# Attention and MLP with a gate on one core: statistics copied right behind their reciprocals, the fourth input tile loaded later, the gate finished a block sooner, the input transposes of two blocks moved to their ends

## The chip, the core and the metric

The kernel runs on one core of one Trainium2 chip. A core has five instruction queues: TensorE (PE: matmuls, with weight loads beside them), VectorE (DVE), ScalarE (ACT), GpSimd (POOL) and SyncE (SP, which here issues nearly all DMAs). Each queue works in the order in which its instructions stand; what one engine needs of another it waits for by a semaphore. The metric is the device time of one execution in microseconds (us), lower is better. Before the change three executions took 2256.01, 2258.34 and 2260.13 us, a median of 2258.34.

## What is computed

The reference takes x of 2048 tokens by 576 values, float32. A gate mixes two branches of the same x:

```python
g = sigmoid((x * gate_w).sum(-1, keepdims=True))
# A: softmax attention, 32 heads of 18 values
qkv = (x @ wqkv).reshape(B, S, 3, H, Dh)          # wqkv 576 x 1728
p = softmax(q @ k^T * Dh ** -0.5)
a = (p @ v) @ wo
# B: layer norm, then an MLP of 4608 hidden values
y = (x - mean(x)) / sqrt(var(x) + 1e-5)
b = gelu(y @ w1 + b1) @ w2 + b2
return g * a + (1 - g) * b
```

The kernel keeps float32 accuracy with matmuls on rounded operands: a tensor is split into a rounded high part (named hh, or the first of a pair) and the rest (hl), and each product is made of three matmuls.

## The kernel before

**Stages.** The program has three. The first, some 239 us, is the input stage, and most of the change lies in it: four blocks of 512 tokens (tb = 0 to 3), each with 17 steps (g = 0 to 16) on PE. Steps 0 to 8 are QK groups (qk_group: 14 matmuls of 128x512 into one PSUM tile, then ACT makes hh of it, L886, DVE makes hl, L887, and SP stores both in DRAM, L889 and L890). Steps 9 to 16 are V groups (v_group: 14 matmuls of 128x288; an even one's PSUM is evicted by ACT, an odd one's by DVE, L912, after which SP stores V, L915). The second stage is a loop of 512 steps over heads and key tiles, in which attention and MLP are interleaved on PE by a list of due times. The third, some 49 us, is the output projection (L1203), in four blocks.

**What each block prepares for the next.** While block tb runs, the tile of block tb+1 is loaded (load_x, L733 and L736, two buffers) and goes through these, each called behind the matmuls of one step:

- norm(tb+1, 0) and norm(tb+1, 1): means and variances on DVE (L846, L847), then at the end of the second a square root on ACT (L853) and two reciprocals on DVE (the last is L859), which gives the deviations, 128x4;
- stat_rows: the means and deviations are copied by DVE into one tile, stp (L825, L826), PE transposes it (L828), ACT copies the rows (L829) and SP writes them to DRAM (L830);
- load_wide: SP reads these rows back, spread over all partitions (L834), into a tile that the code calls wide and that the trace names qa;
- norm(tb+1, 2) and norm(tb+1, 3): DVE multiplies the tile by the gate's weights and sums (L866), for the gate;
- x_chunk 0 to 4: PE transposes 128 columns of the tile (L757); DVE subtracts the means (L772, which needs wide), ACT rounds the transposed part (L774), DVE makes the rest (L775); of the last chunk ACT makes two pieces (L778, L779) and DVE half a piece (L780); POOL multiplies by the deviations (L782). The next block's groups multiply with what L774 to L780 write (the tile big);
- y_parts: some steps after its chunk ("lag"), ACT and POOL split the normalized y (L797, L798), and SP stores it (L789, L791) for the MLP.

Block 0 does its own tile besides: norm(0, 0) and norm(0, 1) at g=3 and 4, the gate and the normalization in place at g=7 and 8, and its transposes y_chunk (L805, L806) at g=12 to 16. The weights of Q, K and V come in seven slices, loaded by SP (L743 to L745) and split by ACT and DVE or POOL (L751, L752) ahead of the groups that need them.

**The table of steps.** BLOCK (L59) gives for each of the first three blocks the step of each of these: stats, rows, wide, x (the first chunk), gate, load (of the tile after next) and the lag. PE's PSUM pool of this stage (ps_a) has four tiles, which turn in order. Between the steps stand rounds of attention scores for the loop's first unit (ROUNDS, L54): four matmuls (L227), each with a maximum on DVE (L229). In block 3 the gate is finished: ACT's exponential at g=9 (L988), three small operations of DVE at g=14 (L990 to L992).

**The output stage.** Each of its blocks of 512 tokens has eight half tiles. PLAN (L49) says behind which of them DVE and ACT do the seven pieces (normed 0 to 6) that prepare the block after it.

Of the kernel before, what the change touches and what calls it, by code (L numbers as in the profile page):

```python
# [11 lines left out]
ALU = mybir.AluOpType  # L12
# [35 lines left out]
TOTAL = NB * NG * (G // 2 * 27 * 231 + 8 * 3 * G * 131)  # L48
PLAN = [[(), (0,), (1,), (2,), (3,), (4,), (5, 6), ()], [(), (), (0,), (1,), (2,), (3,), (4,), (5, 6)],  # L49
        [(), (), (0,), (1,), (2,), (3,), (4,), (5, 6)]]  # L50
LAST = 28
# [6 lines left out]
N_AT = {3: 0, 4: 1, 7: 2, 8: 3}  # L58
BLOCK = [dict(stats=0, rows=4, wide=5, x=9, lag=3, gate=15, load=16),  # L59
         dict(stats=2, rows=5, wide=6, x=7, lag=2, gate=13, load=1),  # L60
         dict(stats=0, rows=3, wide=4, x=6, lag=2, gate=12)]
W_AT = {0: 1, 1: 2, 2: 3, 4: 4, 6: 5, 7: 6}
# [6 lines left out]
def gated_mix_kernel(ctx: ExitStack, tc: tile.TileContext, x, wqkv, wo, w1, b1, w2, b2, gate_w, out):  # L69
# [635 lines left out]
    with ExitStack() as a:  # L705
# [117 lines left out]
        def stat_rows(tb):  # L823

            nc.vector.tensor_copy(stp[:, 0:4], stats[:, 4 * tb:4 * tb + 4, 0])  # L825
            nc.vector.tensor_copy(stp[:, 4:8], rstds[tb])  # L826
            ps = psum(ps_a)
            nc.tensor.transpose(ps[:, :P], stp, ident)  # L828
            nc.scalar.activation(strow, ps[:8, :P], AF.Copy)  # L829
            nc.sync.dma_start(st_scr[tb], strow)  # L830
# [7 lines left out]
        def norm(tb, stage):  # L838
# [9 lines left out]
            if stage == 1:  # L848
# [9 lines left out]
                nc.vector.tensor_scalar(sd, sd, 0.5, None, op0=ALU.mult)  # L858
                nc.vector.reciprocal(rstd, sd)  # L859
            if stage >= 2:  # L860
                if stage == 2:
# [75 lines left out]
        for tb in range(NB):  # L937
            work = [(qk_group, (tb, mt)) for mt in (range(9) if tb < 2 else (4, 0, 1, 2, 3, 5, 6, 7, 8))] + [(v_group, (tb, t, n)) for t in range(4) for n in range(2)]
            for g, (fn, args) in enumerate(work):
# [34 lines left out]
                if tb == NB - 1:  # L974
# [7 lines left out]
                    if g == 9:  # L982
# [3 lines left out]
                        next(stream[0])  # L986

                        nc.scalar.activation(gate, glog, AF.Exp, scale=-1.0)  # L988
                    if g == 14:
                        nc.vector.tensor_scalar(gate, gate, 1.0, None, op0=ALU.add)  # L990
                        nc.vector.reciprocal(gate, gate)
                        nc.vector.tensor_scalar(gate1, gate, -1.0, 1.0, op0=ALU.mult, op1=ALU.add)  # L992
                    if g == 7:
# [8 lines left out]
                if tb == 2 and g == 10:  # L1002
                    for c0, c1 in ((0, 3), (3, 5)):
                        dma_r(nc.sync, low[0:64, c0:c1], y_scr[0, 1, c0:c1].rearrange("c p n -> p c n"))
                        defer(6, lambda c0=c0, c1=c1: nc.scalar.activation(low[64:128, c0:c1], low[0:64, c0:c1], AF.Copy))
                if tb == 2 and g == 4:
                    load_k(0, 2 * TB, 3 * TB)
# [310 lines left out]
```

## Time and profile before

The profiled execution took 2257.29 us, its span on the core 2255.4 us. Stretches of it, cut where PE's first matmul of a block stands; busy time is the sum of instructions, the clock is the mean that was granted to PE:

| stretch (us) | length | PE | DVE | ACT | POOL | PE clock | DMA share |
|---|---|---|---|---|---|---|---|
| start, 0 to 9.27 | 9.27 | 4.29 | 2.12 | 3.85 | 8.35 | 1.00 | 0.85 |
| block 0, to 68.08 | 58.81 | 51.80 | 38.08 | 25.78 | 22.56 | 0.94 | 0.75 |
| block 1, to 130.47 | 62.39 | 54.65 | 34.84 | 14.20 | 14.77 | 0.92 | 0.76 |
| block 2, to 188.12 | 57.65 | 55.73 | 42.62 | 15.57 | 12.72 | 1.00 | 0.54 |
| block 3, to 239.42 | 51.30 | 51.30 | 29.89 | 18.59 | 10.95 | 1.00 | 0.69 |
| loop, to 2206.60 | 1967.18 | 1958.28 | 1475.12 | 1343.23 | 934.25 | 1.00 | 0.42 |
| output, to 2255.40 | 48.80 | 44.10 | 25.46 | 7.37 | 0.00 | 1.00 | 0.54 |

A stretch in which PE is busy for its whole length is set by PE. In block 0 it is idle for 7.0 us, in block 1 for 7.7, in block 2 for 1.9. The quoted rows below come from three views. In the timeline a row has start, duration, engine, line, operation, out<-in, shapes and a count; in brackets the idle time of the engine before it and what ended it. In the list of waits a row has the total, the number and the longest. In the windows a row has the stretch, its length, busy time (with the number of instructions) of PE, its weight loads, DVE, ACT and POOL, then PE's clock, DMA's share and GB/s.

### The profile page before, as it was taken

How to read it: one execution, taken by the hardware profiler on the slowest of the kernel's cores; microseconds unless marked ns; L12 is line 12 of the kernel's file. 1: busy time of each engine (PE TensorE's matmuls, PEld its weight loads, DVE VectorE, ACT ScalarE, POOL GpSimd, SP SyncE). 2: the span in 40 equal slices, each digit the busy share in tenths (PEclk: the TensorE clock that was granted, in tenths of full speed). 3: DMA queues.
4: the chain of work that ended last, by engine and by line, in shares of the span. 5: the costliest groups of instructions: out<-in, count | busy, mean ns of one | idle time of the engine just before them, and what ended most of it. 6: DMA issues, size and time to landing. Idle time of an engine off the chain costs nothing.

```text
span 2255.4 us, 51587 instructions
## 1 busy us (share of the span) xinstructions
PE 2220.2 (98%) x20528; PEld 1582.7 (70%) x20528; DVE 1648.1 (73%) x2886; ACT 1428.6 (63%) x2653; POOL 1003.6 (44%) x1001
## 2 busy tenths in 40 slices
PE   8899999999999999999999999999999999999999
PEld 6777766767666767676667666676766767667668
DVE  5476677777777777777777777777776777777734
ACT  3322776777776666666666666666665666666772
POOL 3221756666665444444463444444444444444710
PEclk9999999999999999999999999999999999999999
DMA  8847654444456533333254423243364323342264
GB/s 236 261 165 242 213 175 154 149 143 153 139 193 174 160 103 117 115 128 122 99 154 138 167 99 120 100 139 103 116 172 149 106 99 113 109 131 94 100 220 166
DMA packets 164104, 329.23 MB, mean 146 GB/s; under 512 B 56814, under 2 KB 84074, under 8 KB 153134
## 3 DMA queue, kind: packets, MB, share of 16 engines
q1 hardware_dynamic: 161766, 322.19, 44.3%
q8 instruction: 162, 2.65, 0.5%
q10 hardware_dynamic: 1968, 3.70, 0.4%
q14 instruction: 80, 0.66, 0.1%
q0 software_dynamic: 128, 0.03, 0.0%
HBM read 233.47 MB, written 96.17 MB: 146 GB/s over the span
## 4 chain that ended last, share of the span: by engine, by line
PE 91%; DVE 4%; DMA 2%; ACT 1%; issue 1%; POOL 1%; SPq 0%; ACTq 0%; POOLq 0%; DVEq 0%
PE ps L285 20%; PE ps L484 19%; PE ps L572 19%; PE ps L267 13%; PE ps L227 10%; PE ps L880 3%; PE ps L1203 3%; DVE m L229 1%; PE ps L901 1%; DMA x<-in_B_w_dram 1%; ACT zz L537 0%; POOL w L180 0%; PE ps L757 0%; DMA qk_scr<-hh 0%; ACT p L270 0%
## 5 line engine op out<-in xcount | busy, mean ns | idle before, releaser
L229 DVE TENSOR_REDUCE m<-ps 128x1 f32<-128x512 f32 x2048 | 1312.4, 685 | 407.1 <-PE ps L227 383.2
L270 ACT ACTIVATE p<-ps 128x512 f32<-128x512 f32 x1368 | 741.8, 596 | 381.3 <-PE ps L267 376.8
L484 PE MATMUL ps<-big,w 64*128 64x512 f32 x3708 | 567.9, 393 | 1.9 <-ACT p L270 1.1
L180 POOL TENSOR_SCALAR zz<-zz 128x512 f32<-128x512 f32 x288 | 178.4, 620 | 748.9 <-ACT zz L537 734.0
L270 ACT ACTIVATE ring<-ps 128x512 f32<-128x512 f32 x680 | 369.1, 596 | 188.9 <-PE ps L267 186.3
L572 PE MATMUL ps<-w,hh 64*128 64x288 f32 x4352 | 483.3, 294 | 1.9 <-DVE x L589 0.9
L267 PE MATMUL ps<-qa,ka 56*128 56x512 f32 x2048 | 459.3, 421 | 3.5 <-ACT p L270 1.8
L572 PEld LDWEIGHTS ps<-w,hh 64*128 64x128 f32 x4352 | 424.0, 186 | 29.4 <-DVE x L589 3.0
L227 PE MATMUL ps<-ka,qa 54*128 54x512 f32 x2048 | 436.1, 398 | 0.9
L484 PEld LDWEIGHTS ps<-big,w 64*128 64x128 f32 x3708 | 368.2, 186 | 68.5 <-ACT p L270 1.4
L180 POOL TENSOR_TENSOR zz<-zz,z 128x512 f32<-128x512 f32 x288 | 371.8, 1291 | 24.0
L267 PEld LDWEIGHTS ps<-qa,ka 56*128 56x128 f32 x2048 | 213.0, 184 | 221.7 <-DVE m L229 181.8
L572 PE MATMUL ps<-w,hl 64*128 64x288 f32 x2176 | 347.6, 292 | 0.8 <-POOL hl L180 0.8
L285 PE MATMUL ps<-p,vt 128*32 128x512 f32 x2560 | 322.8, 598 | 0.0
L227 PEld LDWEIGHTS ps<-ka,qa 54*128 54x128 f32 x2048 | 218.8, 185 | 27.3 <-DVE m L229 7.3
L572 PEld LDWEIGHTS ps<-w,hl 64*128 64x128 f32 x2176 | 230.7, 184 | 1.2 <-POOL hl L180 1.1
L180 POOL TENSOR_TENSOR hl<-zz,hh 128x512 fp32r<-128x512 f32 x136 | 176.6, 1299 | 11.3
L180 POOL TENSOR_TENSOR w<-x,w 128x576 fp32r<-128x576 f32 (+1 forms) x54 | 98.8, 1844 | 171.5 <-ACT w L392 144.3
L285 PE MATMUL ps<-ring,vt 128*32 128x512 f32 x1280 | 168.7, 598 | 0.0
L285 PEld LDWEIGHTS ps<-p,vt 128*32 128x32 f32 x2560 | 67.0, 109 | 142.9 <-issue 136.6
L880 PE MATMUL ps<-big,wqk 128*128 128x512 f32 x432 | 110.4, 403 | 0.4 <-DVE wqk L752 0.4
L589 DVE SCALAR_TENSOR_TENSOR x<-ps,x 128x288 f32<-128x288 f32 x256 | 104.1, 449 | 8.6 <-PE ps L572 8.4
(124 smaller groups left out, 1497.8 us busy)
## 6 DMA issues: line engine op xcount, KB each, us to landing
w<-w_scr SPq DMA_DIRECT2D x54, 1152.0 KB
w<-w_scr SPq DMA_DIRECT2D x108, 576.0 KB
x<-in_B_w_dram SPq DMA_DIRECT2D x72, 288.0 KB
w_scr<-w SPq DMA_DIRECT2D x18, 1152.0 KB
w_scr<-w SPq DMA_DIRECT2D x36, 576.0 KB
qa<-qk_scr SPq DMA_DIRECT2D x192, 72.0 KB
ka<-qk_scr SPq DMA_DIRECT2D x84, 144.0 KB
qk_scr<-hh SPq DMA_DIRECT2D x36, 256.0 KB
```

Of the source, the lines that this page charges most:

```text
L180: fn(*args, **kw)
L227: nc.tensor.matmul(ps, qa[r0:r0 + 54, t * P:(t + 1) * P], ka[r0:r0 + 54, kb * TB:(kb + 1) * TB], start=True, stop=True)
L229: nc.vector.tensor_reduce(M4[u][:, h, t, kb:kb + 1], ps, axis=AX.X, op=ALU.max)
L267: nc.tensor.matmul(ps[h], ka[r0:r0 + 56, kc * P:(kc + 1) * P], qa[r0:r0 + 56, qb * TB:(qb + 1) * TB], start=True, stop=True)
L270: nc.scalar.activation(RING[n % 3][:, qb, h], ps[h], AF.Exp, scale=SCALE)
L285: nc.tensor.matmul(OB[u][r:r + 32, :], v[:, k, 19 * h:19 * h + 32], RING[c % 3][:, qb, h, :], start=(k == 0), stop=(k == NT - 1))
L484: nc.tensor.matmul(ps[h], wt[w_][r, c, :], y[r, c, :], start=(k == 0), stop=(k == 26))
L572: mm = nc.tensor.matmul(ps[nn][:, :ND], h_[r, tok], w_[p_][r, cs[nn]], start=(k == 0), stop=(k == 6 * G - 1))
L589: nc.vector.scalar_tensor_tensor(dst, ps[nn][:, :ND], 0.5, b2b[:, cs[nn]] if g == 0 else dst, op0=ALU.mult, op1=ALU.add)
L880: nc.tensor.matmul(ps, w_[:, c, ms], big[:, s_, :], start=(k == 0), stop=False)
L901: nc.tensor.matmul(ps[:, :ND], big[:, s_, tok], w_[:, c, cs], start=(k == 0), stop=False)
L1203: nc.tensor.matmul(ps[:, :ND], OT[b][2][:, s_, tok], w_part(w_, c)[:, cs], start=(k == 0), stop=(k == 13))
```

## The change

```diff
--- before.py
+++ after.py
@@ -46,8 +46,8 @@
 TAIL = (6, 12, 16, 20)
 BUSY = 20
 TOTAL = NB * NG * (G // 2 * 27 * 231 + 8 * 3 * G * 131)
-PLAN = [[(), (0,), (1,), (2,), (3,), (4,), (5, 6), ()], [(), (), (0,), (1,), (2,), (3,), (4,), (5, 6)],
-        [(), (), (0,), (1,), (2,), (3,), (4,), (5, 6)]]
+PLAN = [[(), (0,), (1,), (2,), (3,), (4,), (5, 6), ()], [(), (0,), (1,), (2,), (3,), (4,), (5, 6), ()],
+        [(), (), (0,), (1,), (2,), (3, 4), (5,), (6,)]]
 LAST = 28
 PSTEP = (489, 492, 495, 497)
 ORDER = (0, 1, 3, 2)
@@ -56,9 +56,9 @@
 SLOTS = [lambda g: 0, lambda g: 0, lambda g: int(g >= 4), lambda g: 1 if g < 9 else 2]
 SKIP = 0
 N_AT = {3: 0, 4: 1, 7: 2, 8: 3}
-BLOCK = [dict(stats=0, rows=4, wide=5, x=9, lag=3, gate=15, load=16),
-         dict(stats=2, rows=5, wide=6, x=7, lag=2, gate=13, load=1),
-         dict(stats=0, rows=3, wide=4, x=6, lag=2, gate=12)]
+BLOCK = [dict(stats=0, rows=3, wide=4, x=10, lag=4, gate=15, load=16),
+         dict(stats=6, rows=9, wide=10, x=12, lag=3, gate=8, load=10),
+         dict(stats=0, rows=3, wide=4, x=6, lag=3, gate=4)]
 W_AT = {0: 1, 1: 2, 2: 3, 4: 4, 6: 5, 7: 6}
 W_CUT = (0, 128, 416, 704, 992, 2 * D, 3 * D - 288, 3 * D)
 NSTEP = 512
@@ -822,8 +822,6 @@
 
         def stat_rows(tb):
 
-            nc.vector.tensor_copy(stp[:, 0:4], stats[:, 4 * tb:4 * tb + 4, 0])
-            nc.vector.tensor_copy(stp[:, 4:8], rstds[tb])
             ps = psum(ps_a)
             nc.tensor.transpose(ps[:, :P], stp, ident)
             nc.scalar.activation(strow, ps[:8, :P], AF.Copy)
@@ -857,6 +855,9 @@
                 nc.vector.tensor_add(sd, sd, rstd)
                 nc.vector.tensor_scalar(sd, sd, 0.5, None, op0=ALU.mult)
                 nc.vector.reciprocal(rstd, sd)
+                if tb > 0:
+                    nc.vector.tensor_copy(stp[:, 0:4], stats[:, ts_, 0])
+                    nc.vector.tensor_copy(stp[:, 4:8], rstd)
             if stage >= 2:
                 if stage == 2:
                     junks[tb] = pp.tile([P, 2, 2, TB], F32, name="p").rearrange("p a b c -> p (a b c)")
@@ -984,12 +985,6 @@
                         wp1 = mstack.enter_context(tc.tile_pool(name="m_w1", bufs=3))
                         wp2 = mstack.enter_context(tc.tile_pool(name="m_w2", bufs=4))
                         next(stream[0])
-
-                        nc.scalar.activation(gate, glog, AF.Exp, scale=-1.0)
-                    if g == 14:
-                        nc.vector.tensor_scalar(gate, gate, 1.0, None, op0=ALU.add)
-                        nc.vector.reciprocal(gate, gate)
-                        nc.vector.tensor_scalar(gate1, gate, -1.0, 1.0, op0=ALU.mult, op1=ALU.add)
                     if g == 7:
                         ps = psum(ps_a)
                         nc.tensor.transpose(ps[:, :NFC], b1r, ident[:NFC, :NFC])
@@ -1003,6 +998,12 @@
                     for c0, c1 in ((0, 3), (3, 5)):
                         dma_r(nc.sync, low[0:64, c0:c1], y_scr[0, 1, c0:c1].rearrange("c p n -> p c n"))
                         defer(6, lambda c0=c0, c1=c1: nc.scalar.activation(low[64:128, c0:c1], low[0:64, c0:c1], AF.Copy))
+                if tb == 2 and g == 14:
+                    nc.scalar.activation(gate, glog, AF.Exp, scale=-1.0)
+                if tb == 2 and g == 16:
+                    nc.vector.tensor_scalar(gate, gate, 1.0, None, op0=ALU.add)
+                    nc.vector.reciprocal(gate, gate)
+                    nc.vector.tensor_scalar(gate1, gate, -1.0, 1.0, op0=ALU.mult, op1=ALU.add)
                 if tb == 2 and g == 4:
                     load_k(0, 2 * TB, 3 * TB)
                 for _ in range(ROUNDS[tb](g)):
```

Four things are done. The two copies into stp move from stat_rows into norm, behind the last reciprocal (in block 0 only for the tile that is prepared, not for the block's own). The table BLOCK has new steps: in block 0 rows and wide a step sooner and the chunks a step later; in block 1 the statistics at g=6 instead of 2, the chunks at g=12 to 16 instead of 7 to 11, the gate products at 8 and 9 instead of 13 and 14, the fourth tile loaded at 10 instead of 1; in block 2 the gate products at 4 and 5 instead of 12 and 13. The lags become 4, 3 and 3. The gate is finished in block 2 (g=14 and 16) instead of block 3 (g=9 and 14). In the output stage, which the title leaves out, PLAN does the pieces for the third block one half tile sooner, and the fifth and sixth piece for the fourth one sooner.

The line numbers of the changed kernel differ from those before by one to three; the names stay. On DVE in block 0, from the last reciprocals on (sd and rstd belong to the tile whose statistics stand ahead), the order before was:

```order
L855 RECIPROCAL rstd<-sd 128x4
L856 TENSOR_TENSOR rstd<-rstd,var 128x4
L857 TENSOR_TENSOR sd<-sd,rstd 128x4
L858 TENSOR_SCALAR sd<-sd 128x4
L859 RECIPROCAL rstd<-sd 128x4
L825 COPY stp<-stats 128x4
L826 COPY stp<-rstd 128x4
L887 TENSOR_TENSOR hl<-ps,hh 128x512 x2
L752 TENSOR_TENSOR wv_128<-p,wv_127 128x5x288
```

These reciprocals were those of block 0's own tile, the second set in the queue. Now, on DVE in block 0, the copies stand behind the first set, that of the next block's tile:

```order
L853 RECIPROCAL rstd<-sd 128x4
L854 TENSOR_TENSOR rstd<-rstd,var 128x4
L855 TENSOR_TENSOR sd<-sd,rstd 128x4
L856 TENSOR_SCALAR sd<-sd 128x4
L857 RECIPROCAL rstd<-sd 128x4
L859 COPY stp<-stats 128x4
L860 COPY stp<-rstd 128x4
L888 TENSOR_TENSOR hl<-ps,hh 128x512 x2
L844 BN_STATS st_339<-x 128x6 x2
```

Two evictions and the own tile's statistics, which stood ahead of the copies, now stand behind them.

On SP in block 1, around the statistics on their way out (st_scr) and back (qa<-st_scr; ka and the other qa are loads for the scores), before:

```order
L889 DMA qk_scr<-hh 128x512
L890 DMA qk_scr<-hl 128x512
L830 DMA st_scr<-strow 8x128
L136 DMA qa_104<-qk_scr 18x1024 x6
L136 DMA ka_107<-qk_scr 18x512 x6
L889 DMA qk_scr<-hh 128x512
L890 DMA qk_scr<-hl 128x512
L834 DMA qa_106<-st_scr 128x1024
```

Now, on SP at the same two transfers:

```order
L890 DMA qk_scr<-hh 128x512
L891 DMA qk_scr<-hl 128x512
L828 DMA st_scr<-strow 8x128
L136 DMA ka_107<-qk_scr 18x512 x6
L916 DMA v_scr<-vt_109 128x780
L733 DMA x<-in_A_x_dram 128x4x576
L736 DMA x<-in_A_x_dram 128x4x64
L832 DMA qa_106<-st_scr 128x1024
L916 DMA v_scr<-vt_110 128x780
```

The pair has moved behind all nine QK groups, and a V store and the fourth tile's two loads stand between.

On DVE at the end of block 1, from the fourth chunk on (p<-ps is the subtraction of the means, big what the next block multiplies with, m a maximum of scores), before:

```order
L772 TENSOR_TENSOR p<-ps,qa_106 128x512
L775 TENSOR_TENSOR big<-ps,big 128x512
L772 TENSOR_TENSOR p<-ps,qa_106 128x512
L780 TENSOR_TENSOR big<-ps,hh 64x512
L229 TENSOR_REDUCE m_1067<-ps 128x1 x4
L912 COPY vt_110<-ps 128x8x2x18
L866 SCALAR_TENSOR_TENSOR p,glog<-x,gwb 128x576 x2
L229 TENSOR_REDUCE m_1067<-ps 128x1 x4
L912 COPY vt_109<-ps 128x8x2x18
L866 SCALAR_TENSOR_TENSOR p,glog<-x,gwb 128x576 x2
L229 TENSOR_REDUCE m_1067<-ps 128x1 x4
```

Now, on DVE from the fourth chunk of the same block on:

```order
L772 TENSOR_TENSOR p<-ps,qa_106 128x512
L775 TENSOR_TENSOR big<-ps,big 128x512
L229 TENSOR_REDUCE m_1035<-ps 128x1 x4
L913 COPY vt_110<-ps 128x8x2x18
L772 TENSOR_TENSOR p<-ps,qa_106 128x512
L780 TENSOR_TENSOR big<-ps,hh 64x512
L888 TENSOR_TENSOR hl<-ps,hh 128x512
L844 BN_STATS st_1293<-x 128x6 x2
```

The last chunk is now followed by block 2's first group; the gate products and all four sets of maxima stand ahead of it.

## The prediction

> **What bounds the kernel now.** I read the page's busy times first, then the list of who waited for whom on PE in the first 240 us, then the timelines of PE, DVE and SP there.
>
> ```profile
> PE 2220.2 (98%) x20528; PEld 1582.7 (70%) x20528; DVE 1648.1 (73%) x2886; ACT 1428.6 (63%) x2653; POOL 1003.6 (44%) x1001
> ...
> PE ps L828 <- DVE stp L826: 9.1, 3, 5.7
> PE ps L757 <- DVE big L775: 5.9, 1, 5.9
> ```
>
> PE is busy 98% of the span of 2255.4 us, so only its idle time, 35 us, and its slow time can be won by a change of order. The waits (total us, times, longest) are in the input part: three transposes of means and deviations (L828) stood 9.1 us behind the copies into stp, and one transpose of the input 5.9 us behind DVE.
>
> ```profile
> 26.71 0.39 PE L883 MATMUL ps<-big,wqk 128*128 128x512 f32 x1
> 32.84 0.45 PE L828 MATMUL ps<-ident,stp 128*128 128x128 f32 x1 [5.75 <-DVE stp L826]
> 32.94 4.72 PE L880 MATMUL ps<-big,wqk 128*128 128x512 f32 x12
> 68.08 3.04 PE L880 MATMUL ps<-big,wqk 128*128 128x512 f32 x12
> 89.69 0.33 PE L828 MATMUL ps<-ident,stp 128*128 128x128 f32 x1 [1.76 <-DVE stp L826]
> 108.41 1.09 PE L757 MATMUL ps<-ident,x 128*128 128x128 f32 x4 [5.86 <-DVE big L775]
> 130.47 2.96 PE L880 MATMUL ps<-big,wqk 128*128 128x512 f32 x12
> 146.17 0.33 PE L828 MATMUL ps<-ident,stp 128*128 128x128 f32 x1 [1.62 <-DVE stp L826]
> ```
>
> Block 1 runs from 68.08 to 130.47 (62.4 us), block 2 to 188.12. A whole group of L880 to L883 takes 3.27 us. After the 5.75 us of idling twelve matmuls took 4.72 us instead of the 2.96 at 130.47: the clock was down. The columns below end in PE's granted clock, the share of DMA and GB/s:
>
> ```profile
> 28.00:30.00 2.00, 0.00 (x0) 0.00 (x0) 1.93 (x7) 0.00 (x0) 2.00 (x2) 0.95 0.26 25
> 34.00:36.00 2.00, 2.00 (x6) 1.59 (x5) 0.00 (x0) 0.00 (x0) 0.00 (x0) 0.50 1.08 157
> 72.00:74.00 2.00, 2.00 (x11) 1.58 (x9) 1.37 (x4) 0.23 (x1) 0.00 (x0) 1.00 1.03 394
> 114.00:116.00 2.00, 2.00 (x14) 1.98 (x13) 2.00 (x4) 0.00 (x0) 0.82 (x1) 0.71 0.00 0
> ```
>
> So each of the two long waits also cost some microseconds at half clock (the second until about 115, by the mean of 0.71 there); the waits of 1.7 us did not.
>
> **Block 0: the copies.** They wait for nothing but the second reciprocal of the tile they belong to, and stood in DVE's queue behind the other tile's statistics.
>
> ```profile
> 24.50 0.18 DVE L859 RECIPROCAL rstd<-sd 128x4 f32<-128x4 f32 x1
> 32.53 0.16 DVE L826 COPY stp<-rstd 128x4 f32<-128x4 f32 x1
> 25.04 5.14 POOL L752 TENSOR_TENSOR wqk<-p,wqk 128x1440 fp32r<-128x1440 f32 x2 [13.24 <-DMA qk_scr<-hh]
> 34.35 0.59 SPq L745 DMA_DIRECT2D p<-in_A_wqkv_dram  x1
> 41.99 1.40 ACT L751 ACTIVATE wv<-p 128x1440 fp32r<-128x1440 f32 x1
> 43.42 1.66 DVE L752 TENSOR_TENSOR wv<-p,wv 128x1440 fp32r<-128x1440 f32 x1 [0.61 <-ACT wv L751]
> 51.91 0.68 DVE L772 TENSOR_TENSOR p<-ps,qa 128x512 f32<-128x512 f32 x1
> ```
>
> Moved behind the reciprocal of 24.50 they end at about 24.9. The transpose now comes a group sooner, at 23.7 (26.71 + 0.25 less one group), so PE waits there 1.3 us, runs the fifth group to 28.3, and starts the sixth at once: the first of POOL's two subtractions, which it needs, ends about then (5.14 us for 1440 and 800 columns, 3.3 of it for the first). That is 32.94 - 28.3 = 4.6 us sooner, and 1.8 more for the clock: 6.4. But it does not last. The last slice of the V weights is issued up to 34.35 and is behind nothing that moves; it had landed by 41.99, and I put it at 40. ACT's 1.40 and DVE's 1.66 follow, so DVE's two halves of the input's gate and normalization start 2 us sooner, not 6.4, and the first subtraction (L772) at about 50.3 with one V copy more ahead of it. DVE sets the pace from there (its chunks come every 1.95 us), PE has one V group more behind it by then, and walking the two in turn, each PSUM tile waiting for the fourth before it, I end block 0 at 65.0 instead of 68.08. **-3.0**, bounds -2.0 (DVE alone) and -6.4.
>
> **Block 1: transposes at the end.** With g for the step and T for the block's start. The statistics now follow the groups g=6 and 7 and end with the copies at T+31.2, while PE reaches their transpose at T+31.6: no wait (1.76 gone). What is late next is the broadcast of the statistics (L832, "wide"), and it sets the block's end.
>
> ```profile
> 92.06 0.28 SPq L830 DMA_DIRECT2D st_scr<-strow  x1
> 100.83 0.43 SPq L834 DMA_DIRECT2D qa<-st_scr  x1
> 106.21 0.69 DVE L772 TENSOR_TENSOR p<-ps,qa 128x512 f32<-128x512 f32 x1 [8.26 <-DMA qa<-st_scr]
> 109.26 2.17 SPq L136 DMA_DIRECT2D ka<-qk_scr  x6
> 75.36 1.03 SPq L733 DMA_DIRECT2D x<-in_A_x_dram  x1
> 82.38 0.82 DVE L846 BATCH_NORM_STATS2 st<-x 128x6 f32<-128x288 f32 x2 [2.90 <-DMA x<-in_A_x_dram]
> 180.12 0.76 DVE L866 SCALAR_TENSOR_TENSOR p<-x,gwb 128x576 f32<-128x576 f32 x1
> 112.68 2.48 DVE L229 TENSOR_REDUCE m<-ps 128x1 f32<-128x512 f32 x4
> ```
>
> On SP it stands behind the six ka pieces (2.2 us), the first V store and the fourth tile's two loads (1.5 us). The V store waits for DVE's copy, and that copy now stands behind an eviction, the four gate products that moved here (0.8 each undisturbed) and four maxima (2.48): 31.2 + 0.7 + 3.3 + 2.5 + 0.4 = T+38.1. SP then issues the loads and at T+40.2 the broadcast. Issue to use took 5.4 us before (100.83 to 106.21), which gives T+45.6; a whole tile took 7.0 (75.36 to 82.38), so the one ahead lands at about T+45.6 and the 512 KB behind it by T+47 or 48. I take T+46.5. DVE wants it at T+41, after the next four maxima and copy.
>
> By the Trainium skill, page DMA: Bandwidth & Descriptors, section Queues, rings and completion order, each engine takes the descriptors of one queue in ring order, so the broadcast's data come after the whole tile; by that the late end of these bounds is the likelier, and the sum would be 1 us longer.
>
> Behind the broadcast DVE works in order: five chunks, two times four maxima, two V copies.
>
> ```profile
> 53.26 0.69 DVE L775 TENSOR_TENSOR big<-ps,big 128x512 fp32r<-128x512 f32 x1 [0.67 <-ACT big L774]
> 119.50 0.69 DVE L780 TENSOR_TENSOR big<-ps,hh 64x512 fp32r<-64x512 f32 x1 [1.19 <-ACT big L779]
> ```
>
> A chunk is 0.68 + 0.67 + 0.69 less overlap, 1.95; the last 2.6. Together 4 x 1.95 + 2.6 + 2 x 2.45 + 0.9 = 16.2, so the last chunk is ready 16.4 us after the broadcast. Before, the gate products and three of the four sets of maxima stood behind the last chunk, where PE did not wait for them. Block 2's first group needs that chunk for its last two matmuls, 2.8 us in; so block 2 starts, in effect, at T + 46.5 + 16.4 + 0.5 - 3.3 = T+60.1 instead of T+62.4: **-2.3**, one microsecond for each of the broadcast's. The fourth tile itself is wanted only in block 2, some 17 us after it lands, and the halves of y that slip into block 2 are read by the loop alone; their stores make 1024 KB for each of five groups, 320 GB/s by 3.27 us, below the 394 reached at 72 to 74. Both cost nothing; were that DMA too slow, each group would wait a few tenths.
>
> PE idles for about 3 us before the third chunk and some 4 us in that first group. The nearest rows, 5.75 and 5.86 us, brought half clock, 1.76 did not. Bounds 0 and 3.3 (half of the 6.7 us from PE's restart at 108.41 to full clock at about 115); **+2.0**.
>
> The Trainium skill, page TensorE: Matmul & The Clock Gate, section What's actually happening, says that the clock halves after an idle window of about 3.4 us and that the windows run free. The trace went to half less than 3 us into the wait that began at 27.1 (0.95 in 28 to 30), which is shorter than that window. By the rule as written the first wait would cost nothing and the second only by luck; the sum would be 2 us less.
>
> **Block 2 and the loop's start.**
>
> ```profile
> 162.08 0.73 PE L227 MATMUL ps<-ka,qa 54*128 54x512 f32 x4
> 184.10 2.13 PE L227 MATMUL ps<-ka,qa 54*128 54x512 f32 x4
> 236.62 2.36 DVE L992 TENSOR_SCALAR gate<-gate 128x16 f32<-128x16 f32 x1
> 239.63 1.09 PE L267 MATMUL ps<-qa,ka 56*128 56x512 f32 x2 [0.21 <-DVE m L229]
> 241.29 0.45 DVE L912 COPY vt<-ps 128x288 f32<-128x288 f32 x1
> 241.84 0.97 PE L484 MATMUL ps<-big,w 64*128 64x512 f32 x6 [1.12 <-ACT p L270]
> ...
> PE ps L1203 <- DVE big L1132: 0.8, 2, 0.4
> ...
> L988 ACT ACT_TABLE_LOAD x1 | 1.3, 1283 | 0.0
> ```
>
> The copies stand ahead of a set of maxima and two evictions: at T2+11.7 against PE's T2+14 (1.62 gone). The gate products move from among the V groups, where the last score round took 2.13 instead of 0.73, to the QK groups, where two groups and a round take PE 7.3 us and DVE 7.1: 1.4 gone. **-3.0** (bounds -1.6, if the round still waits, and -4). At the loop's start the three small gate operations held DVE from 235.27 to 238.9; PE's first MLP matmul at 241.84 follows the V copy that ends at 241.74, not the ACT it is put down to. Without them both small waits go, **-1.3**; in block 2 the same three, and ACT's table load (1.3 us if nothing covered it), stand among V groups, where ACT has every second eviction only. The pieces for the third output block, and the fifth and sixth for the fourth, come half a tile sooner: both waits of 0.4 go, **-0.8** (0 if the last row sums land late).
>
> Sum against the span: 2255.4 - 3.0 - 2.3 + 2.0 - 3.0 - 1.3 - 0.8 = 2247.0. The profiled execution took 2257.29, 1.9 more than its span, so 2248.9; the median of the runs is 1.05 above that execution: **2250 us**.
>
> **Rivals.** One: more is kept. Block 0 keeps all 6.4, because the last weight slice lands before PE wants it (nothing shows when it landed, only that it had by 41.99); a transfer need not wait out the tile ahead of it, so the broadcast lands 3.8 us after SP issues it, at T+44; and the clock stays up: 2250 - 3.4 - 2.5 - 2 = 2242. Against it: the broadcast took 5.4 before without a tile ahead, and SP's wait for the V copy cannot be shortened by transfers. Two: what is won early is given back. Block 0 keeps only DVE's 2.0 and the broadcast lands 5 us later than I say, since the V store and the tile share the queue: 2250 + 1 + 5 = 2256, no change that can be told. Three, slower: the broadcast alone, over a serial chain of 16.4 us. From 8.3 us behind my T+46.5, so 22 us after its statistics leave for DRAM at T+32.8, block 1 eats everything; at 13 us late the time is 2263. Before, that path took 14.1 us (92.06 to 106.21) with twelve loads between, now six loads, a store and a tile; so it would need DMA as crowded as at 80 to 92, and nothing in the order puts that there.
>
> **How the numbers follow.** Forecast 0.55, rival one 0.18, two 0.20, three 0.07. A measurement here tells 0.2%, 4.5 us, from no change. The forecast's own range is 2244 to 2255: block 0 at 6.4 or 2.0, clock 0 or 3.3, broadcast 2 sooner or 3 later, not all on one side. With the rivals: 2242 to 2258. Faster: 0.50 of the forecast, rival one, and a quarter of two, 0.73; slower 0.07; within 0.20.
>
> **What would show it.** PE's wait at the first stp transpose about 1.3, and none at the other two; no half clock before 100 us; DVE waiting at L772 for the broadcast about 5 us, in block 1 only; PE waiting some 4 us in block 2's first group for L780; from first to first group, block 0 takes 55.7 us, block 1 some 56 and block 2 some 61, with its first wait and the clock in it. Wrong if the wait in block 1 is far from 5 us, if PE stands before block 1, or if the loop, which nothing here touches, changes its 1967 us.

## The result and the profile after

The changed kernel takes **2250.39 us**, the median of six runs (2246.34 to 2250.67), against 2258.00 for six runs of the kernel before beside it (2256.01 to 2260.13). The ratio is 0.9963, with a 95% interval of 0.9950 to 0.9976: 0.24 to 0.50% faster. The profiled execution took 2250.38, its span 2248.6 us (2255.4 before).

The page's busy times, and then the list of who waited for whom on PE in the first 240 us, with the one wait of the output stage as its last line:

```profile
PE 2219.2 (99%) x20528; PEld 1585.2 (70%) x20528; DVE 1643.9 (73%) x2886; ACT 1426.9 (63%) x2653; POOL 1003.9 (45%) x1001
...
PE ps L883 <- DVE big L780: 3.6, 1, 3.6
PE ps L757 <- ACT v L911: 3.1, 1, 3.1
PE ps L902 <- DVE vt L913: 2.1, 1, 2.1
PE ps L826 <- DVE stp L860: 1.2, 1, 1.2
...
PE ps L1204 <- ACT big L1128: 0.6, 1, 0.6
```

The copies' waits have gone from 9.1 us to 1.2 (L826 is now the transpose of the statistics), and so has the 5.9 us at L757 behind L775. In their place stand waits for the last chunk (L780), and at L757 behind ACT: ACT's V copy stands in its queue behind L774, which in turn waits for DVE's L772. The rows of the changed kernel's timeline that carry the rest:

```profile
25.18 0.30 PE L826 MATMUL ps<-ident,stp 128*128 128x128 f32 x1 [1.20 <-DVE stp L860]
40.38 1.41 ACT L751 ACTIVATE wv<-p 128x1440 fp32r<-128x1440 f32 x1 [4.40 <-DMA p<-in_A_wqkv_dram]
50.26 0.68 DVE L772 TENSOR_TENSOR p<-ps,qa 128x512 f32<-128x512 f32 x1
50.40 3.15 PE L902 MATMUL ps<-wv,big 128*128 128x288 f32 x12 [2.13 <-DVE vt L913]
65.42 3.05 PE L881 MATMUL ps<-big,wqk 128*128 128x512 f32 x12
97.77 0.30 SPq L828 DMA_DIRECT2D st_scr<-strow  x1
104.71 0.69 SPq L832 DMA_DIRECT2D qa<-st_scr  x1
112.21 0.69 DVE L772 TENSOR_TENSOR p<-ps,qa 128x512 f32<-128x512 f32 x1 [6.28 <-DMA qa<-st_scr]
112.93 0.60 ACT L774 ACTIVATE big<-ps 128x512 fp32r<-128x512 f32 x1 [10.55 <-DVE p L772]
113.98 0.66 PE L757 MATMUL ps<-ident,x 128*128 128x128 f32 x4 [3.14 <-ACT v L911]
121.45 3.05 PE L881 MATMUL ps<-big,wqk 128*128 128x512 f32 x12
127.36 0.69 DVE L780 TENSOR_TENSOR big<-ps,hh 64x512 fp32r<-64x512 f32 x1 [1.14 <-ACT big L779]
128.11 0.50 PE L883 MATMUL ps<-big,wqk 128*128 128x512 f32 x1 [3.61 <-DVE big L780]
128.68 4.50 PE L881 MATMUL ps<-big,wqk 128*128 128x512 f32 x12
178.76 0.73 PE L227 MATMUL ps<-ka,qa 54*128 54x512 f32 x4
181.37 2.96 PE L881 MATMUL ps<-big,wqk 128*128 128x512 f32 x12
233.28 0.97 PE L484 MATMUL ps<-big,w 64*128 64x512 f32 x6 [0.17 <-issue]
2161.98 1.58 PE L1204 MATMUL ps<-big 128*128 128x288 f32 x10
2243.17 0.30 PE L1204 MATMUL ps<-wlast,big 128*128 128x288 f32 x1
```

Block 1 starts at 65.42, block 2 at 121.45, block 3 at 181.37, the loop's first MLP matmul stands at 233.28, the output stage's first and last at 2161.98 and 2243.17 (before: 68.08, 130.47, 188.12, 241.84, 2169.80, 2251.23). From these the whole difference can be cut up:

| stretch | before | after | measured | predicted |
|---|---|---|---|---|
| start of block 0 | 9.27 | 9.19 | -0.1 | 0 |
| block 0 | 58.81 | 56.23 | -2.6 | -3.0 |
| blocks 1 and 2 | 120.04 | 115.95 | -4.1 | -2.3 + 2.0 - 3.0 = -3.3 |
| block 3 to the first MLP matmul | 53.72 | 51.91 | -1.8 | -1.3 |
| from there to the first output matmul | 1927.96 | 1928.70 | +0.7 | 0 |
| first to last output matmul | 81.43 | 81.19 | -0.2 | -0.8 |
| last output matmul to the end of the span | 4.2 | 5.4 | +1.2 | 0 |
| sum | 2255.4 | 2248.6 | -6.8 | -8.4 |

### The profile page after: what moved, and what is told of

Its sections match the earlier page's. It is cut to its first block, busy times and chain, and to the rows that moved or that the text cites. A ratio compares the mean times of both kernels' runs of the same rounds, so it can differ in the third digit from the quotient of the medians.

```text
span 2248.6 us, 51575 instructions
## 1 busy us (share of the span) xinstructions
PE 2219.2 (99%) x20528; PEld 1585.2 (70%) x20528; DVE 1643.9 (73%) x2886; ACT 1426.9 (63%) x2653; POOL 1003.9 (45%) x1001
## 4 chain that ended last, share of the span: by engine, by line
PE 90%; DVE 4%; DMA 2%; ACT 2%; issue 1%; POOL 1%; SPq 0%; ACTq 0%; DVEq 0%; POOLq 0%
PE ps L285 20%; PE ps L572 19%; PE ps L484 19%; PE ps L267 13%; PE ps L227 10%; PE ps L881 3%; PE ps L1204 2%; DVE m L229 2%; PE ps L902 1%; DMA x<-in_B_w_dram 1%; ACT zz L537 0%; POOL w L180 0%; DMA qa<-st_scr 0%; DMA p<-in_A_wqkv_dram 0%; DVE p L772 0%
```

## The experiments

The first column of times is from block 0's first group to block 1's, the second from there to block 3's, the third on to the first MLP matmul; all from the timelines. Before and after are medians of six runs, run 1 of ten, runs 3 and 10 of four; the others are single times. Single spans differ by some microseconds in code that no edit touches: from the first MLP matmul to the end of the span the twelve profiled executions took 2012.9 to 2015.3 us, the changed kernel's the longest. So the stretches say more than the span.

| kernel | block 0 | blocks 1, 2 | block 3 | span | time |
|---|---|---|---|---|---|
| before | 58.81 | 120.04 | 53.7 | 2255.4 | 2258.00 |
| after | 56.23 | 115.95 | 51.9 | 2248.6 | 2250.39 |
| 1 copies alone | 57.16 | 117.92 | 53.7 | 2253.0 | 2254.83 (2253.42 to 2255.80) |
| 2 load later still | 55.99 | 112.45 | 51.9 | 2243.5 | 2245.23 |
| 3 broadcast early | 56.32 | 111.35 | 51.9 | 2241.6 | 2242.17 (2240.61 to 2243.40) |
| 4 gate products sooner | 53.64 | 114.37 | 51.9 | 2243.6 | 2245.34 |
| 5 maxima ahead | 55.90 | 124.39 | 51.9 | 2254.9 | 2256.96 |
| 6 load at once | 56.97 | 114.92 | 51.9 | 2246.7 | 2248.73 |
| 7 gate products back | 56.71 | 117.03 | 51.9 | 2248.0 | 2249.75 |
| 8 gate and plan back | 56.33 | 114.69 | 53.7 | 2248.5 | 2250.28 |
| 9 maxima to block 3 | 55.89 | 109.58 | 53.7 | 2241.5 | 2243.27 |
| 10 all three | 53.65 | 103.14 | 53.6 | 2233.3 | 2235.11 (2234.69 to 2235.66) |

**1. The copies alone**, in the kernel before:

```diff
 def stat_rows(tb):
-    nc.vector.tensor_copy(stp[:, 0:4], stats[:, 4 * tb:4 * tb + 4, 0])
-    nc.vector.tensor_copy(stp[:, 4:8], rstds[tb])
...
     nc.vector.reciprocal(rstd, sd)
+    if tb > 0:
+        nc.vector.tensor_copy(stp[:, 0:4], stats[:, ts_, 0])
+        nc.vector.tensor_copy(stp[:, 4:8], rstd)
```

> The kernel before with one thing of the change: the two copies into stp stand behind the last reciprocal; table of steps, gate and output as before. Theory (block 0's gain comes from the copies, and its size is set by the last V-weight slice that lands at 40 and by DVE behind it, not by the copies): the three waits at the stp transposes (5.7, 1.8, 1.6 us) are all gone, block 0 goes from 58.8 to 55.5-57 us, a wait of 2 to 4 us of PE behind DVE shows near 48-52, block 2 loses 1.6; the whole is 4 to 6 us less, 2252 to 2254. Rival (the copies alone are worth the whole 5.75 wait and its half clock): block 0 at 52.4, the whole 8 to 10 us less, 2248 to 2250, which would mean that the rest of the change is worth nothing. Rival (the copies are worth only their own waits' excess, and the new steps of the table made block 0's gain): block 0 above 58.

Against the kernel before the ratio is 0.9984 (0.9975 to 0.9994), 3.6 us. Block 0 won 1.7 us, a little less than expected, block 2 1.8, block 1 only 0.3. The timeline of this kernel:

```profile
51.97 1.09 PE L757 MATMUL ps<-ident,x 128*128 128x128 f32 x4 [2.56 <-DVE big L775]
...
104.24 0.69 DVE L772 TENSOR_TENSOR p<-ps,qa 128x512 f32<-128x512 f32 x1 [9.06 <-DMA qa<-st_scr]
```

The 5.75 us at the first transpose are gone, but PE stands 2.56 at 51.97 behind DVE, and in block 1 DVE waits 9.06 for the broadcast where it waited 8.26. Of the second transpose's wait 0.7 us is left, and of the 3.8 that the blocks won 1.4 were lost again in the loop's first ten microseconds, where the granted clock was 0.50 from 239.5 to 242.9 in this run and 1.00 at the same place before; so the whole is a little less than the 4 to 6 expected. The copies are worth about half of the change; what blocks 1 and 2 won beyond the copies' 2.1, another 2.0, came from the table of steps.

**2. The fourth tile's load behind the broadcast**, in the changed kernel:

```diff
-         dict(stats=6, rows=9, wide=10, x=12, lag=3, gate=8, load=10),
+         dict(stats=6, rows=9, wide=10, x=12, lag=3, gate=8, load=12),
```

> The changed kernel with load=12 instead of 10 in block 1, so that SP issues the broadcast of the statistics ahead of the fourth tile's two loads (and of nothing else new). Theory (the broadcast sets the end of block 1 through a serial chain on DVE, and its data come behind the tile's in the queue): the broadcast is issued 1.0 us sooner and lands 3 to 4.5 us sooner; DVE's wait at L772 falls from 6.3 to 2-3.5, PE's two waits (3.1 at L757, 3.6 for L780) shrink by as much in all, and blocks 1 and 2 together get 3 to 5 us shorter, 115.9 to 111-113. Rival (transfers do not wait for each other; only the issue counts): it lands 1.0 us sooner and blocks 1 and 2 are 1 us shorter. Rival (block 1 is not set by the broadcast): no change in the blocks' sum.

```profile
103.28 0.43 SPq L832 DMA_DIRECT2D qa<-st_scr  x1
107.56 0.69 DVE L772 TENSOR_TENSOR p<-ps,qa 128x512 f32<-128x512 f32 x1 [1.93 <-DMA qa<-st_scr]
```

From issue to use the broadcast now takes 4.28 us, with the tile ahead of it 7.50 (104.71 to 112.21). The tile cost 3.2 us of landing and 1.1 of issue, and blocks 1 and 2 became 3.5 shorter: theory held, and both rivals fell. Of PE's two waits only the 3.1 at L757 went; the one for L780 stayed, with 3.70.

**3. The broadcast early:**

```diff
-         dict(stats=6, rows=9, wide=10, x=12, lag=3, gate=8, load=10),
+         dict(stats=5, rows=8, wide=9, x=12, lag=3, gate=8, load=10),
```

> The changed kernel with the statistics of block 1 one step sooner (stats 5, rows 8, wide 9 instead of 6, 9, 10): SP then issues the broadcast ahead of the six ka pieces, the first V store and the fourth tile. Theory (late broadcast, serial chain behind it): it is issued at about T+31 and lands at T+36 to T+38, before DVE wants it at T+41; the wait of 6.3 at L772 is gone, L780 ends at about T+57 instead of T+62.6, PE's 3.1 before the third chunk is gone, the wait for L780 falls from 3.6 to 1-2.5, half clock goes with the waits, and blocks 1 and 2 together take 107 to 110 us instead of 115.9; the time is 2241 to 2245. Rival (DVE's chain alone, not its start, sets the pace, or PE at low clock does): blocks 1 and 2 at 114 or more, the time 2249 to 2251.

The time is in the expected range (ratio to before 0.9927, 0.9910 to 0.9943), the blocks are 1.4 us longer than expected. The timeline shows two reasons:

```profile
97.43 0.64 SPq L828 DMA_DIRECT2D st_scr<-strow  x1
102.17 0.32 SPq L832 DMA_DIRECT2D qa<-st_scr  x1
105.77 0.69 DVE L772 TENSOR_TENSOR p<-ps,qa 128x512 f32<-128x512 f32 x1 [0.67 <-DMA qa<-st_scr]
116.16 0.42 ACT L909 ACTIVATE vt<-ps 128x288 f32<-128x288 f32 x1 [2.40 <-DMA v_scr<-vt]
123.63 0.80 PE L883 MATMUL ps<-big,wqk 128*128 128x512 f32 x1 [3.45 <-DVE big L780]
```

SP had issued the store of the statistics by 98.07 and then stood until 102.17, 4.0 us of it put down to the store (L832 <- DMA st_scr<-strow), since the broadcast reads what that store writes; in the changed kernel the ka pieces filled this time. And a new wait took 2.4 us of the gain: ACT's V copy at 116.16 waits for a V store, which now stood right behind the fourth tile in the queue, and the fourth chunk waits behind ACT. The last chunk is ready 17.8 us after the first L772 instead of 15.8.

**4. Block 0's gate products a step sooner:**

```diff
-N_AT = {3: 0, 4: 1, 7: 2, 8: 3}
+N_AT = {3: 0, 4: 1, 6: 2, 7: 3}
```

> The changed kernel with block 0's own first gate products and normalization at g=6 and the second at g=7 (N_AT 6 and 7 instead of 7 and 8), so that half of that DVE work (2.7 us) stands ahead of the last V-weight slice, in the 5.1 us in which DVE waits for it. Theory (block 0 is set by the late slice and by the DVE work behind it): the first L772 comes 2.5 us sooner, at 47.6 instead of 50.3, PE's wait of 2.1 at the second V pair and the half clock at 50 to 54 are gone, and block 0 takes 52 to 53 us instead of 56.2. Rival (the slice holds PE itself, or the DVE pace of 1.95 us per chunk sets the rest of the block): block 0 at 55 or more, with the wait moved behind the next chunk. Blocks 1 and 2 the same in both within 0.5 us.

```profile
47.97 0.68 DVE L772 TENSOR_TENSOR p<-ps,qa 128x512 f32<-128x512 f32 x1
...
125.34 0.51 PE L883 MATMUL ps<-big,wqk 128*128 128x512 f32 x1 [2.66 <-DVE big L780]
125.92 2.96 PE L881 MATMUL ps<-big,wqk 128*128 128x512 f32 x12
```

The first subtraction comes 2.3 us sooner, and block 0 is 2.6 shorter (I had said 3.2 to 4.2). So DVE's work behind the late slice sets block 0's end; the slice's own landing was not varied. Blocks 1 and 2, whose instructions are the changed kernel's, got 1.6 shorter too, against my half a microsecond: after 2.66 us of waiting the twelve matmuls took 2.96, after 3.61 in the changed kernel 4.50.

**5. Three sets of maxima ahead of the broadcast**, with the loads that they need:

```diff
-... lambda g: 2 * (g in (9, 11, 13, 15)), ...
+... lambda g: 2 * (g in (3, 4, 5, 9)), ...
-                if tb == 1 and g == 5:
+                if tb == 1 and g == 1:
                     load_q(0)
                     load_k(0, 0, TB)
```

> The changed kernel with the score rounds of block 1 at steps 3, 4, 5 and 9 instead of 9, 11, 13 and 15 (and the loads of their q and first k at step 1 instead of 5): three of the four sets of maxima leave the place behind the V store or behind the broadcast; the broadcast itself stays where it is on SP, behind the V store and the fourth tile. Theory (what block 2's first group waits for is DVE's serial chain behind the broadcast): the broadcast still lands about 46 to 47 us into the block and DVE still waits 6 us or more at L772, since it has less to do ahead, but from that landing to the last chunk (L780) it takes 10.5 to 11.5 us instead of 15.9; PE's wait of 3.6 for L780 falls to under 0.5, and blocks 1 and 2 together get 3.5 to 5.5 us shorter than 115.9. Rival (the broadcast's landing alone decides, DVE's work behind it does not): the wait for L780 stays above 2.5 and the sum within 1 us of 115.9.

```profile
86.89 0.76 PE L227 MATMUL ps<-ka,qa 54*128 54x512 f32 x1 [8.48 <-DMA ka<-qk_scr]
...
125.63 0.69 DVE L772 TENSOR_TENSOR p<-ps,qa 128x512 f32<-128x512 f32 x1 [8.06 <-DMA qa<-st_scr]
137.01 0.69 DVE L780 TENSOR_TENSOR big<-ps,hh 64x512 fp32r<-64x512 f32 x1 [1.14 <-ACT big L779]
```

The sum of the blocks missed both expectations: q and k were not there so early, and PE stood 8.48 us for them. The chain itself came near to what the theory said: from the landing to the end of the last chunk 12.1 us (125.63 to 137.70; 10.5 to 11.5 expected) instead of 15.8, and no wait for L780 is left. Run 9 asks the same without moving a transfer.

**6. The fourth tile's load back at the start of block 1:**

```diff
-         dict(stats=6, rows=9, wide=10, x=12, lag=3, gate=8, load=10),
+         dict(stats=6, rows=9, wide=10, x=12, lag=3, gate=8, load=1),
```

> One part of the change undone in the changed kernel: the fourth tile's load is back at step 1 of block 1. Theory (the tile ahead of the broadcast costs 1.0 us of issue and 3.2 of landing, as the run with the load at step 12 showed): as there, the broadcast lands 3.5 to 4.5 us sooner than in the changed kernel, PE's 3.1 at L757 is gone, blocks 1 and 2 together take 111 to 113 us instead of 115.9, the span is near 2243.5 to 2245. Rival (the load stood in the way at the block's start too, among the stores of y and the third tile, and moving it was worth something there): the sum of the blocks above 114, with a new wait of PE in the first ten microseconds of block 1 or late statistics of the third tile.

```profile
101.04 0.70 SPq L828 DMA_DIRECT2D st_scr<-strow  x1
107.35 0.43 SPq L832 DMA_DIRECT2D qa<-st_scr  x1
112.07 0.69 DVE L772 TENSOR_TENSOR p<-ps,qa 128x512 f32<-128x512 f32 x1 [3.17 <-DMA qa<-st_scr]
```

The sum of 114.92 lies on the rival's side, though not with its signs: the statistics were in time, but SP came 2.6 us later to their store (34.96 into the block instead of 32.35) and PE waited 1.2 us for ka. The broadcast took 4.7 from issue to use, as expected without the tile, but left 2.0 later. So moving the load was worth something on SP, and the place chosen, just ahead of the broadcast, cost more: 1.0 in all, and 3.5 against the place two steps later.

**7. Block 1's gate products back among the chunks:**

```diff
-         dict(stats=6, rows=9, wide=10, x=12, lag=3, gate=8, load=10),
+         dict(stats=6, rows=9, wide=10, x=12, lag=3, gate=13, load=10),
```

> One part of the change undone in the changed kernel: block 1's four gate products back at steps 13 and 14. Theory (serial chain): the V copy comes about 1 us sooner (the maxima wait for their scores by then), and the broadcast with it, but the four products, 3.2 us, now stand between the chunks, so the last chunk is ready 18.5 to 19.5 us after the broadcast's landing instead of 15.9; PE waits 1.5 to 3 us longer in all, blocks 1 and 2 together take 117 to 119 us instead of 115.9. Rival (the products ahead of the V store were what made the broadcast late, all 3.2 us): the sum unchanged or below 115.9.

```profile
111.20 0.69 DVE L772 TENSOR_TENSOR p<-ps,qa 128x512 f32<-128x512 f32 x1 [5.41 <-DMA qa<-st_scr]
129.31 0.69 DVE L780 TENSOR_TENSOR big<-ps,hh 64x512 fp32r<-64x512 f32 x1 [1.14 <-ACT big L779]
```

From the landing to the end of the chain 18.8 us instead of 15.8, the landing 1.6 us sooner in the block (45.1 instead of 46.8), the blocks 1.1 longer: the lower end of what the theory said. That the span is 0.6 shorter all the same comes from later stretches in which nothing was changed (the loop 0.9, the output stage 0.6 and the end of the span 0.8 shorter).

**8. The gate's finish and the output's table as before:**

```diff
-                if tb == 2 and g == 14:
+                if tb == 3 and g == 9:
                     nc.scalar.activation(gate, glog, AF.Exp, scale=-1.0)
-                if tb == 2 and g == 16:
+                if tb == 3 and g == 14:
...
-PLAN = [...], [(), (0,), (1,), (2,), (3,), (4,), (5, 6), ()],
-        [(), (), (0,), (1,), (2,), (3, 4), (5,), (6,)]]
+PLAN = [...], [(), (), (0,), (1,), (2,), (3,), (4,), (5, 6)],
+        [(), (), (0,), (1,), (2,), (3,), (4,), (5, 6)]]
```

> Two parts of the change undone in the changed kernel: the gate is finished in block 3 again (steps 9 and 14), and the output stage has its old table of pieces. Theory: from block 3's first group to the loop's matmuls it takes 1.3 to 1.8 us longer, with the 1.1 us wait at the loop's first MLP matmul back; block 2 is at most 0.3 us shorter; in the output, PE's two waits of 0.4 are back, and from the first to the last output matmul it takes 0.2 to 0.8 us longer. Rival (the gate's finish was hidden in both places, the loop takes up what it is given): the distance from block 3's first group to the 16th MLP pair is the same within 0.3 us.

```profile
128.52 0.50 PE L883 MATMUL ps<-big,wqk 128*128 128x512 f32 x1 [2.67 <-DVE big L780]
129.09 2.96 PE L881 MATMUL ps<-big,wqk 128*128 128x512 f32 x12
...
233.99 0.97 PE L484 MATMUL ps<-big,w 64*128 64x512 f32 x6 [1.12 <-ACT p L270]
```

The 1.12 us are back and block 3 to the first MLP matmul takes 1.8 longer; as expected. The output stage takes 81.60 instead of 81.19, with its two waits of 0.4 back; that is in the expected range too, but less than the stage differs between executions with one table (below). The span shows nothing of it, since blocks 1 and 2, unchanged up to the gate, ran 1.3 us shorter: here PE kept its clock after the wait for L780.

**9. Two sets of maxima to block 3**, no transfer moved:

```diff
-... lambda g: 2 * (g in (9, 11, 13, 15)), ...
+... lambda g: 2 * (g in (9, 11)), ...
-          lambda g: 2 * (g in (4, 5, 6, 7, 8, 10, 12, 14))]
+          lambda g: 2 * (g in (0, 1, 4, 5, 6, 7, 8, 10, 12, 14))]
```

> The changed kernel with the two later score rounds of block 1 (steps 13 and 15, the two sets of maxima behind the broadcast) moved to block 3 (steps 0 and 1), with no transfer moved; PE gives away 1.35 us in block 1 and gets it back in block 3. The run with the maxima ahead moved the loads of q and k too, and its 8.5 us of waiting for them hid what it was made for. Theory (serial chain of DVE behind the broadcast): the broadcast lands 46 to 47.5 us into block 1 as in the changed kernel, with DVE's 6.3 us wait and PE's 3.1 at L757; from the landing to the end of the last chunk 11 to 12.3 us instead of 15.8; PE's wait for L780 under 1 instead of 3.6; blocks 1, 2 and 3 together 162.5 to 164.5 us instead of 167.2, the span 2243.5 to 2246. Rival (the landing alone decides, or the maxima cost in block 3 what they saved): the three blocks within 1 us of 167.2.

```profile
111.57 0.69 DVE L772 TENSOR_TENSOR p<-ps,qa 128x512 f32<-128x512 f32 x1 [6.07 <-DMA qa<-st_scr]
122.09 0.69 DVE L780 TENSOR_TENSOR big<-ps,hh 64x512 fp32r<-64x512 f32 x1 [1.14 <-ACT big L779]
```

The landing is where it was (46.6 into the block, with DVE's wait of 6.07), the chain takes 11.2 us, no wait for L780 is left, and the three blocks took 162.6 us instead of 167.2 (block 3 to the loop's first matmul). The serial chain is shown. The span is 2 us below what I expected, by as much won behind the loop's start, in stretches that were not changed.

**10. All of it together:** the edits of 4 and 9, block 0's rows and wide a step later, block 1's statistics as in 3 with the tile's load at step 14.

```diff
-BLOCK = [dict(stats=0, rows=3, wide=4, x=10, lag=4, gate=15, load=16),
-         dict(stats=6, rows=9, wide=10, x=12, lag=3, gate=8, load=10),
+BLOCK = [dict(stats=0, rows=4, wide=5, x=10, lag=4, gate=15, load=16),
+         dict(stats=5, rows=8, wide=9, x=12, lag=3, gate=8, load=14),
```

> The changed kernel with every cause named so far taken away: in block 0 the gate products and normalization a step sooner (g=6 and 7) and the transpose of the statistics a step later (rows 4, wide 5, so that PE reaches it behind the copies); in block 1 the statistics a step sooner (5, 8, 9) so that the broadcast leaves ahead of the ka pieces and the V store, the fourth tile loaded at step 14, behind three V stores; the two later rounds of maxima in block 3. Theory: block 0 takes 52.3 to 53.8 us instead of 56.2, blocks 1 and 2 together 104.5 to 107 instead of 115.9 with no wait of PE over 1 us and full clock throughout, block 3 52.5 to 53 instead of 51.2; the time is 2236 to 2240. Rival (PE's own work or DMA already sets these blocks, the single gains do not add): 2241 or more.

```profile
PE 2212.6 (99%) x20528; PEld 1577.1 (71%) x20528; DVE 1644.0 (74%) x2886; ACT 1427.9 (64%) x2653; POOL 1006.0 (45%) x1001
...
102.39 0.69 DVE L772 TENSOR_TENSOR p<-ps,qa 128x512 f32<-128x512 f32 x1
113.46 0.69 DVE L780 TENSOR_TENSOR big<-ps,hh 64x512 fp32r<-64x512 f32 x1 [1.14 <-ACT big L779]
```

2235.11 us, a ratio to before of 0.9895 (0.9878 to 0.9911), beats both kernels, and my range by 0.9. PE waits for nothing in blocks 1 and 2; DVE's first L772 has no wait before it. The single gains add up: runs 4 (block 0), 3 and 9 (the blocks behind it) won 2.6, 4.6 and 4.6 us, 11.8 together, and here the four blocks up to the first MLP matmul are 13.7 shorter.

## Why the prediction was right, point by point

**Block 0 (-3.0, measured -2.6): right in mechanism and place.** The wait at the first transpose is 1.20 (1.3 predicted), the last weight slice was there at 40.38 (40), the first L772 stands at 50.26 (50.3). DVE set the pace from there: run 4 took 2.3 us of work from in front of that L772 and the block fell by 2.6. Rival one's 6.4 could not be kept by moving copies.

**Block 1 and the broadcast (-2.3): right.** Issued 39.3 us into the block (40.2), landed at 46.8 (46.5), DVE waited 6.3 (5 to 5.5), and the chain behind it took 15.8 (16.4). Runs 2, 7 and 9 show the parts: where landing and chain together ended 4.4 us sooner, 1.3 later and 4.9 sooner, blocks 1 and 2 became 3.5 shorter, 1.1 longer and 6.4 shorter (about 1.4 of it the two rounds that left block 1), nearly one for one. The sentence that the fourth tile costs nothing held for its use in block 2; in the queue it cost 4.3 us (run 2), which the forecast had in its landing time. The Trainium skill (DMA: Bandwidth & Descriptors, section Queues, rings and completion order) has each engine consume the descriptors of one queue in ring order. With that, 7.50 us behind the tile against 4.28 without it agrees.

**The clock (+2.0): right in size for the wait for L780, partly by luck, and wrong as a rule.** After 3.61 us the twelve matmuls took 4.50 instead of 2.96, 1.5 us; what was lost after the wait at 113.98 fell into the wait for L780. But "no half clock before 100 us" was wrong: it came at 50.5, behind a wait of 2.13 us, where the forecast had only asked whether a wait was nearer to 1.7 or to 5.8. It cost next to nothing there, since DVE set the pace: with the clock at full behind the same wait (run 2, below) PE waited 1.0 us more at the next tile, and block 0 took 55.99 instead of 56.23. The luck is in the place of the wait: in run 8, with the same instructions up to there, PE waited 2.67 us for L780 and kept its clock, and nothing of the 2.0 was paid behind that wait.

**Block 2 (-3.0): right.** Both waits of the stp transposes are gone, the last score round took 0.73 (178.76) instead of 2.13. Without its first wait and clock, block 2 took 59.92 - 3.61 - 1.54 = 54.8 us, against 57.65 before: -2.9.

**The loop's start (-1.3, measured -1.8): right, and shown by undoing it (run 8).**

**The output (-0.8, measured -0.2): right in mechanism, too large for this execution.** The two waits of 0.4 went, but a wait of 0.6 behind ACT's L1128 came in the fourth block. The other traces show both: the three executions with the old table (before, runs 1 and 8) have the two waits and take 81.4 to 81.6 us; none of the nine with the new one has them. Six of these take 80.4 to 80.7, which is 0.7 to 1.2 less and so around the 0.8 that was forecast; the other three (the changed kernel's, runs 4 and 10) have a wait of 0.6 to 0.8 behind L1128 and take 81.1 to 81.5. Why that wait comes in some executions only is open.

**What no term had.** From the first MLP matmul to the first output matmul it took 0.7 us more, and the last stores landed 1.2 us later after the last matmul. Neither is in code that the change touches, and both belong to this execution: the twelve traces have 1927.8 to 1929.4 us for the first (run 7, with the same instructions, 0.9 less than the changed kernel's) and 4.2 to 4.6 us for the second in all but this one, 5.4. So the span came out 1.6 us above the sum. That the median agrees to 0.4 us is luck: this profiled execution lay on its median, where I had added 1.05, and that made up for most of it.

**The other signs.** Two of the signs of being wrong need a word. "If PE stands before block 1": at that border there is no wait (none from 60.83 to 65.42), but inside block 0 PE stood 2.13 us at 50.40, which the forecast did not name. "If the loop changes its 1967 us": from its first matmul to the last stretch of output matmuls (239.42 to 2206.55 before, 232.61 to 2198.73 now) it takes 1966.1 us instead of 1967.1, and its start alone became 1.75 shorter, by the waits that the forecast had.

## What to carry to other kernels

When a copy is moved ahead in its queue, look for the next late thing before counting the wait as won: here it was a weight slice in one block and a transfer that reads back a just written row in the next, and each set the end through the serial work behind it. Price a late transfer by what stands ahead of it in its own queue and by what stands behind it on the engine that reads it; both can be shortened without touching the transfer. And look at the order that a change leaves before taking its gain as final: one number of the table, load=12 for load=10, shortened two blocks by 3.5 us, and the three causes together were worth 15 more, twice the change itself.

## What the runs showed of the hardware that I had not expected

The length of a wait does not tell whether the clock falls. Up to the wait behind L913 the block 0 of the changed kernel and of run 2 have the same instructions, and the wait is 2.13 us long in both. The windows view, PE's granted clock third from the end, first the changed kernel:

```profile
50.00:52.00 2.00, 1.60 (x7) 1.60 (x8) 1.34 (x3) 1.00 (x3) 0.84 (x1) 0.63 0.63 184
52.00:54.00 2.00, 2.00 (x11) 1.98 (x10) 1.34 (x3) 0.60 (x1) 1.47 (x2) 0.51 0.33 129
```

Then run 2:

```profile
50.00:52.00 2.00, 1.46 (x11) 1.46 (x12) 1.33 (x4) 0.88 (x3) 0.70 (x1) 1.00 0.64 146
52.00:54.00 2.00, 1.54 (x13) 1.30 (x12) 1.34 (x3) 1.04 (x4) 1.48 (x2) 1.00 0.40 158
```

Half clock behind the one, full clock behind the other; and 2.66 and 2.67 us in runs 4 and 8 cost nothing where 3.61 cost 1.5. The twelve traces show what goes with it. The granted clock in them is 1.00 or 0.50, and it changes only on a grid of 3.41 us: up to the last matmuls, half clock lasts 3.41, 6.83 or 10.24 us. I cut the first 2200 us of each run on its own grid, from 9 us on. At full clock, PE was busy for 1.43 us or less in 21 of these stretches, and behind each of the 21 the next was at half clock. In all other stretches PE was busy for 1.56 us or more, and behind them the clock stayed full but for three (PE busy 2.2 us; run 1 at 236.1, run 6 at 96.7, run 7 at 115.9). Score matmuls ran in these three; why they differ is open.

By that, what counts is how much of a wait falls into one stretch. The 2.13 us lay in one in the changed kernel (47.12 to 50.54, PE busy 1.29 us); in run 2 the wait reached over the border at 50.26, and PE was busy for 1.56 us of the stretch before it. Most of the 3.61 us lay in one (125.63 to 129.04, PE busy 0.93), while run 4's 2.66 us were shared by two (busy 2.35 and 1.82). Where the grid lies differs between executions of the same instructions, so a forecast from the kernel can only give the chance.

The Trainium skill (TensorE: Matmul & The Clock Gate, section What's actually happening) has windows that run free, and half clock after an idle window of about 3.4 us. The grid agrees with the windows; but the window ahead of half clock need not be idle, as the 1.43 us of work in run 4's show (106.68 to 110.10).

A grid that lies differently each time would also make times scatter: the changed kernel's six runs spread over 4.3 us, the four of run 10, in which no wait of more than 0.8 us is left in blocks 0 to 3, over 1.0. That the clock is the cause of that spread is not shown, and the fastest of the six, 2246.34 us, does not owe its time to it: its mean granted clock, 0.997, is no higher than the 0.998 of the other five.

A load that reads what the store just ahead of it writes held SP's queue for 4.1 us in run 3 (98.07 to 102.17) and for 3.1 in run 10 (94.77 to 97.89), for 4 KB. What does not depend on that store can be issued in between, as the six ka pieces were in the changed kernel (98.13 to 101.27).
